# Two late reads of a channel-attention kernel, split by partitions

## The chip, the cores and the metric

One core of one Trainium2 chip runs the kernel. The metric is the device time of one execution in microseconds (us), and the median of several runs is compared.

## What is computed

x has 384 x 384 pixels of 384 channels in bf16 (113 MB). The reference takes a mean and a maximum over all pixels for each channel, sends both through the same two small layers, and scales x by the result:

```
gap = mean(x, pixels)                      # 384 values
gmp = max(x, pixels)                       # 384 values
h_a, h_m = relu(gap @ w1), relu(gmp @ w1)  # w1: 384 x 96
scale = sigmoid(h_a @ w2 + h_m @ w2)       # w2: 96 x 384
out = x * scale                            # per channel
```

No pixel can be written before every pixel was read. x does not fit into the memory beside the engines (SBUF), so there are two passes: one that reads all of x, and one that reads most of it again and writes all of it.

## The kernel before

Pixels are taken in "rows": one row is one pixel on each of 128 partitions, 768 bytes per partition. There are 1152 rows. A read of n rows brings n x 768 bytes in one piece to each partition.

*The first pass* is a list of steps written out by hand (`steps`). Lines 367 to 397 walk through it. For every read, SyncE issues the transfer (line 371); TensorE sums the rows by matmuls against ones (`sums`, line 274; for the last four reads `tail_sums`, line 290); and VectorE takes the maximum with an accumulator `acc` of eleven rows (`maximum`, line 340). VectorE takes up to six or five rows at a time, into two halves of `acc` in turn (`HALVES`), so that an instruction depends on the last but one. ScalarE and TensorE also pack some rows (lines 301 to 329); that is over by 240 us.

*The end of the first pass*, around the change: the last blocks stay in SBUF, so that the second pass need not read them again. `STAYING` gives their reads: 16 and 15 rows (stay 0), 11, 11 and 9 (stay 1), 11, 10, 8 and 5 (stay 2). Then come `LAST_HELD`: 8 rows (the late block), 2 and 6 (the kept block), 5 (the held block). After the reads up to stay 2, `turn_sums` brings the sums into place (lines 284 and 285; its copies use the room of w1 and w2, so both weights are read only afterwards, lines 399 and 400). `turn_over` transposes the late block into PSUM (line 346). Before the maximum of the six kept rows VectorE folds `acc` from eleven rows to six (`fold`); after the five held rows it folds on to one row, which TensorE transposes (line 423) and VectorE reduces (line 424). Two small products (lines 428 and 430) and a sigmoid on ScalarE (line 431) give `scale_bc`. Then SyncE also reads back eight rows (line 415) and the rows that `acc` had displaced (line 412).

*The second pass* multiplies by `scale_bc` on VectorE (line 436). ScalarE issues the stores (lines 445, 451 and 490), SyncE the reads (line 529), each into room that a store has left.

The order on each engine is the order of the program. The framework puts in the semaphore waits: a transfer signals one of eight completion semaphores (DMAHW0 to DMAHW7), taken in turn by all transfers whichever engine issues them, and waits for the one before it on the same semaphore. In the built program the five-row read of stay 2 waits for DMAHW0, the late block for DMAHW1, the kept reads for DMAHW2 and DMAHW3 and the held read for DMAHW4.

Of the kernel before, what the change touches and what calls it, by code (L numbers as in the profile page):

```python
# [39 lines left out]
FIRST_AT = (0, 104, 40, 64, 200, 176, 152)  # L40
# [12 lines left out]

FIRST_LOAD = 4
FOLD_BEFORE = 2

BETWEEN = (
    ((21, 30), (208, 48)), ((51, 21), (0, 49), (72, 21)), ((208, 51), (0, 46), (46, 34)),
# [8 lines left out]
STAYING = ((16, 15), (11, 11, 9), (11, 10, 8, 5))  # L67
# [20 lines left out]
def kernel(  # L88
# [7 lines left out]
    nc = tc.nc  # L96
    P = nc.NUM_PARTITIONS
# [9 lines left out]
    xr = x.rearrange("b h w c -> (b h w) c")  # L107
    orr = out.rearrange("b h w c -> (b h w) c")

    def rows_of(ap, block):  # L110
        first, n = block
        return ap[first * P:(first + n) * P, :].rearrange("(p n) c -> p n c", n=n)
# [7 lines left out]
    def take(n):  # L120
        nonlocal at
        at += n
        return at - n, n
# [3 lines left out]
    packed_block = take(GP * PACKED)  # L127
    late_block, kept_block, held_block = (take(sum(pieces)) for pieces in LAST_HELD)
    stay = [take(n) for _, n in SLOTS]
# [34 lines left out]
    rows = nc.alloc_sbuf_tensor_at("rows", [P, HELD_ROWS + BODY_ROWS, C], BF16, offset=RING_BYTES).ap()  # L164
# [18 lines left out]
    late = words_ps[:, 0:LATE_ROWS, :]  # L183
# [49 lines left out]
    for i in range(PACKED):  # L233
        if i in TOGETHER:
            lo = min(HOME_AT[i], D_AT[i % 2])
# [34 lines left out]
    def sums(rows, n, done, total):  # L270
        for k in range(0, n, MM_ROWS):
            g = min(MM_ROWS, n - k)
            for q in range(CQ):
                nc.tensor.matmul(  # L274
                    sum_ps[q * QP:q * QP + 1, 0:g * P],
                    lhsT=ones_bf[:, 0:1],
                    rhs=rows[:, k:k + g, q * P:(q + 1) * P],
                    start=(done + k == 0),
                    stop=(done + k + g == total),
                )  # L280

    def turn_sums():
        for r in range(MM_ROWS):
            nc.scalar.copy(out=s_sb[r % 2], in_=sum_ps[:, r * P:(r + 1) * P])  # L284
            nc.tensor.matmul(gsum_ps, lhsT=s_sb[r % 2], rhs=pick, start=(r == 0), stop=False)

    def tail_sums(rows, n, last):
        for k in range(n):
            for q in range(CQ):
                nc.tensor.matmul(  # L290
                    gsum_ps[:, q:q + 1], lhsT=rows[:, k, q * P:(q + 1) * P], rhs=ones_bf,
                    start=False, stop=(last and k == n - 1 and q == CQ - 1),
                )
# [12 lines left out]
    def test(i, what):  # L306

        if what == 2:
            test_one(high(part(i, 3), I8), 5 * i + 4)
            return  # L310
        n = G * C // 2
        a_b = homes[i][:, 0:2 * G, :].rearrange("p (r n) c -> p r (n c)", r=2).bitcast(I8)
        test_one(a_b[:, :, 2 * n * what + 1:2 * n * (what + 1):2], 5 * i + 2 * what)
        test_one(high(part(i, 2), I8)[:, n * what:n * (what + 1)], 5 * i + 2 * what + 1)

    def pack(i, half):
        n = G * C // 2
        span = slice(half * n, (half + 1) * n)
        for c in range(0, n, BANK):
            for r in range(4):  # L320
                for k, dt in enumerate((E4, E3)):
                    nc.tensor.matmul(  # L322
                        words[:, c:c + BANK], lhsT=weights[2 * r + k],
                        rhs=high(part(i, r), dt)[:, half * n + c:half * n + c + BANK],
                        start=(r == 0 and k == 0), stop=(r == 3 and k == 1),
                    )
        for r in (0, 1):
            nc.scalar.copy(out=high(part(i, r), U8)[:, span], in_=low(part(i, r + 2), U8)[:, span])  # L328
        nc.scalar.activation(  # L329
            out=part(i, 2).rearrange("p n c -> p (n c)").bitcast(U16)[:, span], in_=words,  # L330
            func=ACT.Copy, bias=32767.5,
        )

    def judge():
        nc.scalar.activation(out=test_copy, in_=tests[:, 0:NT], func=ACT.Copy, accum_out=test_sum)
        nc.scalar.copy(out=total, in_=test_sum)
        nc.tensor.matmul(bad_ps, lhsT=total, rhs=ones_bf, start=True, stop=True)

    def maximum(out_, in0, in1):
        nc.vector.tensor_tensor(out=out_, in0=in0, in1=in1, op=ALU.max)  # L340

    def turn_over(out_, rows):

        for r in range(LATE_ROWS):
            for q in range(CQ):
                nc.tensor.transpose(  # L346
                    out=out_[:, r, q * P:(q + 1) * P], in_=rows[:, r, q * P:(q + 1) * P], identity=ident_bf
                )
# [3 lines left out]
    def fold():  # L352

        n = folds[-1]
        h = n // 2
        maximum(acc[:, 0:h, :], acc[:, 0:h, :], acc[:, n - h:n, :])
        folds.append(n - h)

    done = turn = nth = 0
    for st in steps:  # L360
        if st[0] == "test":
            test(*st[1:])
        elif st[0] == "pack":
            pack(*st[1:])
        elif st[0] == "judge":
            judge()
        if st[0] != "load":
            continue
        _, block, rows, lo, hi = st
        m = hi - lo  # L370
        nc.sync.dma_start(out=rows, in_=rows_of(xr, block)[:, lo:hi, :])  # L371
        if nth < len(loads) - SUM_TAIL:
            sums(rows, m, done, TOT - tail_rows)
        else:
            tail_sums(rows, m, nth == len(loads) - 1)
        if nth == len(loads) - FOLD_BEFORE:
            fold()
        halves = HALVES if len(folds) == 1 else ((0, folds[-1]),)
        j = max(0, min(m, A - done))
        if j:  # L380
            nc.vector.tensor_copy(out=acc[:, done:done + j, :], in_=rows[:, 0:j, :])
        done += m
        if nth == len(loads) - SUM_TAIL - 1:
            turn_sums()
        while j < m:
            c, e = halves[turn % len(halves)]
            turn += 1
            e = min(e, c + m - j)
            maximum(acc[:, c:e, :], acc[:, c:e, :], rows[:, j:j + e - c, :])
            j += e - c  # L390
        if block == late_block:
            turn_over(late, rows)
        elif block == first_block:
            nc.vector.tensor_copy(out=kept_ps.bitcast(U32), in_=rows[:, 0:PSUM_ROWS, :].bitcast(U32))
            nc.vector.tensor_copy(out=kept_b.bitcast(U32), in_=rows[:, PSUM_ROWS:for_psum, :].bitcast(U32))
        nth += 1
# [23 lines left out]
    for q0, part_ps in tp_ps:  # L420
        n = part_ps.shape[1]
# [160 lines left out]
    with tc.If(bad != 0):  # L582
        for i in range(PACKED):
            for buf, lo in ((homes[i], FIRST_AT[i]), (homes_d[i], FOURTH_AT[i])):
                n = buf.shape[1]
# [33 lines left out]
```

## Time and profile before

| What | Value |
|---|---|
| median of 3 runs | 725.81 us (725.53 to 725.83) |
| the profiled execution | 725.41 us, span 723.6 us |
| first pass, up to the scale | 276.2 us |
| second pass | 447.4 us |
| VectorE busy | 564.1 us (78%) |
| ScalarE busy | 349.8 us (48%) |
| TensorE busy | 184.7 us (26%) |
| HBM read, written | 192.14 MB, 113.25 MB; 422 GB/s over the span |
| TensorE clock granted | 0.62 in the mean |

The span runs from the first to the last instruction of the profiled execution; its own time has some 1.8 us around it. A line of a timeline gives the start and the length in us, engine, line of the code, operation, output<-input, sizes and count; in brackets stands how long the engine had been idle before it and what ended that. DVE is VectorE, ACT ScalarE, PE TensorE, PEld its weight loads, SP SyncE; a q marks the engine's queue. "Landing" is the time at which a transfer's last completion event came.

### The profile page before, as it was taken

The page shows a single profiled execution, that of the slowest core. Times are in us where ns is not written, and L with a number is a line of the kernel's source. Part 1 is how long each engine was busy: PE and PEld are TensorE (multiplying, and loading weights), DVE is VectorE, ACT ScalarE, POOL GpSimd, SP SyncE. Part 2 cuts the span into 40 slices and gives each one's busy share as a digit, 9 for nine tenths or more (in the row PEclk, how much of TensorE's full clock was granted, in tenths as well). Part 3 has the DMA queues.
Part 4 walks back from the last instruction along what each step waited for, and adds up shares of the span by engine and source line. Part 5 has one row for each costly group of instructions (what it writes and reads, how often), then busy time and mean ns, then how long its engine had stood idle before and what let it go on. Part 6 is the DMA issues. An engine that isn't in the chain of part 4 may idle for free.

```text
span 723.6 us, 3882 instructions
## 1 busy us (share of the span) xinstructions
PE 184.7 (26%) x1363; PEld 74.2 (10%) x1363; DVE 564.1 (78%) x445; ACT 349.8 (48%) x251; POOL 0.7 (0%) x6
## 2 busy tenths in 40 slices
PE   5577475965867470000000000000000000001000
PEld 1222122322322140000000000000000000001000
DVE  5699899999999998797966554897888889495200
ACT  6999999997999200056230023806154442200000
POOL 0000000000000000000000000000000000000000
PEclk9888878896988555555555555555555555555555
DMA  9999999999999979999999999999999999999997
GB/s 380 434 438 435 417 442 427 429 430 432 431 426 428 426 312 356 400 433 431 433 431 431 434 428 431 434 430 435 430 429 432 437 432 430 430 433 439 442 426 339
DMA packets 20403, 305.63 MB, mean 422 GB/s; under 512 B 2624, under 2 KB 2976, under 8 KB 7200
## 3 DMA queue, kind: packets, MB, share of 16 engines
q1 hardware_dynamic: 13040, 192.14, 62.3%
q10 hardware_dynamic: 7344, 113.25, 36.6%
q8 instruction: 10, 0.16, 0.1%
q14 instruction: 9, 0.07, 0.0%
HBM read 192.14 MB, written 113.25 MB: 422 GB/s over the span
## 4 chain that ended last, share of the span: by engine, by line
DMA 63%; DVE 25%; issue 3%; PE 2%; ACT 1%; SPq 0%; DVEq 0%; ACTq 0%
DMA rows<-in_x_dram 40%; DMA out_dram<-rows 23%; DVE acc L340 16%; DVE rows L436 9%; PE words_ps L322 1%; ACT rows L328 0%; DVE acc L436 0%; SPq L371 0%; PE bank_a L274 0%; ACT rows L329 0%; ACT rows L487 0%; PE bank_a L430 0%; ACT scale_bc L431 0%; DVE small L424 0%; PE bank_a L423 0%
## 5 line engine op out<-in xcount | busy, mean ns | idle before, releaser
L436 DVE TENSOR_TENSOR rows<-rows,scale_bc 128x9216 bf16<-128x9216 bf16 (+9 forms) x56 | 230.9, 4164 | 91.2 <-DMA rows<-in_x_dram 90.0
L340 DVE TENSOR_TENSOR acc<-acc,rows 128x2304 bf16<-128x2304 bf16 (+4 forms) x227 | 245.0, 1154 | 13.9 <-DMA rows<-in_x_dram 13.6
L487 ACT COPY rows<-rows 128x1536 uint8<-128x1536 uint8 x28 | 41.3, 1476 | 204.2 <-DVE rows L436 144.8
L274 PE MATMUL bank_a<-rows,small 128*1 128x512 bf16 (+3 forms) x897 | 93.3, 466 | 80.9 <-DMA rows<-in_x_dram 76.1
L346 PE MATMUL words_ps<-ident_bf,acc 128*128 128x128 bf16 x24 | 2.7, 310 | 376.3 <-DVE acc L574 376.3
L301 ACT ACTIVATE rows<-rows 128x3072 uint8<-128x3072 int8 (+1 forms) x35 | 81.9, 2341 | 9.1 <-DMA rows<-in_x_dram 8.4
L302 ACT ACTIVATE rows<-rows 128x3072 uint8<-128x3072 uint8 (+1 forms) x35 | 82.0, 2344 | 1.1
L487 ACT COPY rows<-acc 128x1536 uint8<-128x1536 uint8 x42 | 60.5, 1473 | 18.2 <-DVE acc L473 17.7
L274 PEld LDWEIGHTS <-small 128*1 128x1 bf16 x897 | 30.6, 95 | 140.3 <-issue 118.2
L346 PEld LDWEIGHTS <-acc 128*128 128x128 bf16 x24 | 2.5, 144 | 376.7 <-DVE acc L574 376.7
L322 PE MATMUL words_ps<-rows,scale_bc 128*128 128x512 fp8e4 (+1 forms) x126 | 37.9, 414 | 9.2 <-ACT rows L329 9.2
L328 ACT COPY rows<-rows 128x1536 uint8<-128x1536 uint8 x28 | 39.7, 1468 | 0.4 <-PE words_ps L322 0.4
L322 PE MATMUL words_ps<-rows 128*128 128x512 fp8e3 (+1 forms) x126 | 35.8, 394 | 0.0
L468 DVE TENSOR_SCALAR rows<-rows 128x1536 uint16<-128x1536 uint16 x56 | 31.3, 560 | 1.9
L322 PE MATMUL words_ps<-rows,w_sb 128*128 128x512 fp8e3 x84 | 27.0, 405 | 0.0
L487 ACT COPY acc<-rows 128x1536 uint8<-128x1536 uint8 x14 | 20.5, 1466 | 0.0
L329 ACT ACTIVATE rows<-words_ps 128x1536 uint16<-128x1536 f32 x14 | 20.1, 1439 | 0.0
L322 PEld LDWEIGHTS <-scale_bc 128*128 128x128 bf16 x126 | 12.2, 103 | 30.2 <-issue 19.3
L322 PEld LDWEIGHTS <-rows 128*128 128x128 bf16 x126 | 12.9, 102 | 16.7 <-issue 3.3
L473 DVE SCALAR_TENSOR_TENSOR acc<-acc,rows 128x768 uint32<-128x768 uint32 x14 | 13.4, 959 | 0.5
L473 DVE SCALAR_TENSOR_TENSOR rows<-rows 128x768 uint32<-128x768 uint32 x14 | 13.4, 958 | 0.5
L284 ACT COPY w_sb<-bank_a 65x128 f32<-65x128 f32 x2 | 0.5, 261 | 24.5 <-PE bank_a L274 24.0
(61 smaller groups left out, 72.0 us busy)
## 6 DMA issues: line engine op xcount, KB each, us to landing
rows<-in_x_dram SPq DMA_DIRECT2D x16, 2880.0 KB, 25.4
out_dram<-rows ACTq DMA_DIRECT2D x15, 2880.0 KB, 22.8
rows<-in_x_dram SPq DMA_DIRECT2D x15, 2304.0 KB, 20.0
out_dram<-rows ACTq DMA_DIRECT2D x14, 2304.0 KB, 21.1
rows<-in_x_dram SPq DMA_DIRECT2D x4, 3072.0 KB, 31.8
out_dram<-rows ACTq DMA_DIRECT2D x2, 4608.0 KB, 46.7
rows<-in_x_dram SPq DMA_DIRECT2D x9, 768.0 KB, 16.7
rows<-in_x_dram SPq DMA_DIRECT2D x2, 3264.0 KB, 26.4
```

The costliest lines, as they stand in the source:

```text
L274: nc.tensor.matmul(sum_ps[q * QP:q * QP + 1, 0:g * P], lhsT=ones_bf[:, 0:1], rhs=rows[:, k:k + g, q * P:(q + 1) * P], start=(done + k == 0 ...
L301: nc.scalar.activation(out=out_, in_=rows, func=ACT.Square, bias=test_bias, scale=TEST_SCALE)
L302: nc.scalar.activation(out=out_, in_=out_, func=ACT.Square, bias=minus4, accum_out=tests[:, k:k + 1],)
L322: nc.tensor.matmul(words[:, c:c + BANK], lhsT=weights[2 * r + k], rhs=high(part(i, r), dt)[:, half * n + c:half * n + c + BANK], start=(r ...
L328: nc.scalar.copy(out=high(part(i, r), U8)[:, span], in_=low(part(i, r + 2), U8)[:, span])
L329: nc.scalar.activation(out=part(i, 2).rearrange("p n c -> p (n c)").bitcast(U16)[:, span], in_=words, func=ACT.Copy, bias=32767.5,)
L340: nc.vector.tensor_tensor(out=out_, in0=in0, in1=in1, op=ALU.max)
L346: nc.tensor.transpose(out=out_[:, r, q * P:(q + 1) * P], in_=rows[:, r, q * P:(q + 1) * P], identity=ident_bf)
L436: nc.vector.tensor_tensor(out=dst, in0=src, in1=scale_bc.unsqueeze(1).to_broadcast([P, n, C]), op=ALU.mult)
L468: nc.vector.tensor_scalar(out=u16(dst), in0=u16(src), scalar1=s1, scalar2=s2, op0=op0, op1=op1)
L473: nc.vector.scalar_tensor_tensor(out=u32(v), in0=u32(v), scalar=0x3F3F3F3F, in1=u32(m), op0=ALU.bitwise_xor, op1=ALU.bitwise_xor)
L487: nc.scalar.copy(out=dst, in_=src)
```

## The change

The two reads are issued in parts: the last five rows of stay 2 as 112 and four times 4 partitions, the late block's eight rows as 96, 12, 12 and 8. Every part brings the same rows to other partitions; nothing else of the first pass is written differently. (`packed` in the loop is a case that the table does not use.)

```diff
 FOLD_BEFORE = 2
+
+UNEVEN = {("stay", 2): (112, 4, 4, 4, 4), ("late", 0): (96, 12, 12, 8)}
...
+    uneven = {}
+    for (kind, i), parts in UNEVEN.items():
+        if kind == "packed":
+            uneven[packed_block, FIRST_AT[i]] = parts
+        elif kind == "stay":
+            uneven[stay[i], sum(STAYING[i][:-1])] = parts
+        else:
+            uneven[late_block, i] = parts
     done = turn = nth = 0
...
         m = hi - lo
-        nc.sync.dma_start(out=rows, in_=rows_of(xr, block)[:, lo:hi, :])
+        a = 0
+        for n in uneven.get((block, lo), (P,)):
+            nc.sync.dma_start(out=rows[a:a + n], in_=rows_of(xr, block)[a:a + n, lo:hi, :])
+            a += n
+        assert a == P
```

In the built program the nine transfers wait, in this order, for DMAHW0 (the 112), 1, 2, 3, 4 (the 4s), 5 (the 96), 6, 7 (the 12s) and 0 again (the 8); the kept and held reads that follow wait for 1, 2 and 3. TensorE's sums and transposes and VectorE's maxima of these rows wait for all parts of their read.

## The prediction

> **What bounds the kernel now.** I read the page first, then stretches around the two changed reads, then the instructions of VectorE and SyncE there one by one, and last the completion events of each transfer.
>
> The page's chain of what ended last:
>
> ```profile
> DMA 63%; DVE 25%; issue 3%; PE 2%; ACT 1%; SPq 0%; DVEq 0%; ACTq 0%
> ```
>
> Transfers lead it, but that is an average over two passes. The change sits in the last 25 us of the first pass, so that stretch decides:
>
> ```profile
> core 0: us, PE busy (x) PEld busy (x) DVE busy (x) ACT busy (x) POOL busy (x), PEclk, DMA share, GB/s
> 228.00:241.50 13.50, 6.39 (x77) 2.37 (x75) 12.69 (x12) 12.08 (x12) 0.00 (x0) 0.82 1.01 426
> 241.60:258.00 16.40, 9.33 (x67) 2.70 (x63) 16.40 (x16) 0.00 (x0) 0.00 (x0) 0.50 1.01 425
> 258.00:268.00 10.00, 7.77 (x72) 4.49 (x72) 10.00 (x11) 0.95 (x4) 0.00 (x0) 0.50 0.86 343
> ```
>
> From 241.6 us VectorE is busy without a break (16.40 of 16.40, then 10.00 of 10.00). It last waited for a read at 241.56:
>
> ```profile
> 241.56 26.48 DVE L340 TENSOR_TENSOR acc<-acc,rows 128x1920 bf16<-128x1920 bf16 x26 [0.87 <-DMA rows<-in_x_dram]
> 268.07 1.16 DVE L340 TENSOR_TENSOR acc<-acc 128x1920 bf16<-128x1920 bf16 x1
> 269.26 2.61 DVE L340 TENSOR_TENSOR acc<-acc,rows 128x2304 bf16<-128x2304 bf16 x2
> 271.90 1.54 DVE L340 TENSOR_TENSOR acc<-acc 128x1152 bf16<-128x1152 bf16 x3
> ```
>
> The line at 268.07 is the first fold (acc into acc); the two at 269.26 take the six kept rows and, from 270.71, the five held rows, the last read; 271.90 is the last three folds. Then come the scale, ready at 276.18, and the second pass. So the pass ends on a chain of VectorE work, each piece behind the one before.
>
> Are the reads late for it? In the semaphore events of the trace each read has sixteen, and the sixteenth is its landing. The reads at stake landed, and were taken by VectorE, at: five rows of stay 2: 263.42 and 264.68; late eight: 265.33 and 265.75; kept two: 265.82 and 267.49; kept six: 267.16 and 269.26; held five: 268.33 and 270.71. A waited-for landing needs about 0.09 us to become an instruction (241.47 to 241.56), so the margins are 1.2, 0.33, 1.6, 2.0 and 2.3 us. **The late block has the small one: it may land up to 265.66.**
>
> SyncE's queue (line 371 issues every read):
>
> ```profile
> 245.13 0.33 SPq L371 DMA_DIRECT2D rows<-in_x_dram  x1
> 245.55 0.38 SPq L371 DMA_DIRECT2D rows<-in_x_dram  x1
> 245.99 0.42 SPq L371 DMA_DIRECT2D rows<-in_x_dram  x1
> 248.57 0.33 SPq L371 DMA_DIRECT2D rows<-in_x_dram  x1
> 251.04 0.33 SPq L371 DMA_DIRECT2D rows<-in_x_dram  x1
> 253.54 0.33 SPq L371 DMA_DIRECT2D rows<-in_x_dram  x1
> 255.65 0.33 SPq L371 DMA_DIRECT2D rows<-in_x_dram  x1
> ...
> 266.57 1.64 SPq L400 DMA_DIRECT2D scale_bc<-in_w_dram  x1
> ```
>
> 245.99 is the five-row read, 248.57 the late block, then kept two, kept six, held five. Each of the last four starts 0.01 to 0.07 us after an earlier read landed (248.51, 251.02, 253.53, 255.58): the one eight transfers before it. The built program shows why: transfers take eight completion semaphores in turn, and one waits until the last user of its semaphore has landed. **At most eight transfers are under way.** They are issued 13 to 17 us ahead of their landing, so waits here cost nothing now.
>
> **The change part by part.**
> *Removed and added.* Two issues of 128 partitions become nine: 112+4+4+4+4 partitions of five rows, 96+12+12+8 of eight. The bytes are the same. The seven extra issues cost SyncE 0.33 to 0.42 us each, 2.3 to 2.9 us in all; SyncE waits for landings from 256 to 266 us, so this is hidden, if the new order of waits allows. VectorE gets three waiting instructions more, TensorE a few; one takes 0.02 us on VectorE's queue, which runs ahead of 1.15 us maxima: nothing.
>
> *The new order of issues.* The depth of eight is now spent on small parts. With the landings of before: 112 partitions at 245.99; the 4s at 248.57, 251.04, 253.54, 255.65; the 96 when the eleven-row read lands, 258.15, so 258.19; the 12s at 260.49 and 262.29 (landings 260.46, 262.26). The 8 waits for the 112. One partition of five rows takes an engine 149 ns (eight take 1.17 us), and every engine has seven instead of eight, so the 112 land at 263.42 - 0.15 = 263.28, and the 8 are issued at 263.31. An issue that meets an idle queue has its first packet 0.98 us later (line 415, 269.74 to 270.72); its packet takes 234 ns, and landing follows a last packet by 0.3 us (same read, 273.62 to 273.94). **The late block is complete at 263.31 + 1.0 + 0.23 + 0.3 = 264.85, earlier than before (265.33) and 0.8 us ahead of 265.66.**
>
> *What is queued behind.* Kept two, kept six and held five go out at 263.7, 264.2 and 264.6, no longer 10 us ahead. The engine that is first ended the eight-row read ahead of the change at 259.17 and has at most 3.74 us more (below), so it is empty from 262.9 on; the last one is not before 264.7. Then the thirteen rows take 13 x 0.234 = 3.04 us from about 264.8: kept two land near 265.6, kept six 267.1, held five 268.2, each within 0.3 us of before, with 1.6 us or more to spare. The weights behind them wait for TensorE (L285, 266.07) in any case. From there on the order is the same with the semaphores shifted by one, so the second pass follows the scale.
>
> *Which engines carry the parts.* No row of the trace shows it for 4, 8 or 12 partitions. The sixteen events of the late block in before run from 262.19 to 265.33, and the spread is 3.1 us in every read from 245 on: some engines are ahead, one is 1.1 us behind all others. Nearest rows: 128 and 96 partitions (weights) both left sixteen events, equal shares of 8 and 6. I take one partition to an engine. An engine with a share of everything then has 11 x 0.149 + 9 x 0.234 = 3.74 us to do after 262.26 if it is the one behind (8 each before: 3.06); one with the least has 7 x 0.149 + 6 x 0.234 = 2.45. If the slow engine has the most, the late block lands at 266.0: +0.35 us. If the least, nothing. Far end: all 48 partitions of the small parts on one engine, 1.04 + 16 x 0.149 + 1.40 + 32 x 0.234 = 12.3 us after 262.26, landing at 274.6: +8.9 us. The other end, spread as before: 0. I take 0.
>
> The Trainium skill (DMA: Bandwidth & Descriptors, on why a DMA increments its semaphore by 16) states that a transfer runs on the largest number of engines up to sixteen that divides its partitions, the lowest-numbered ones; by it the 4s share four engines, the 12s twelve, the 8 eight, and the sum stays 0 or +0.35.
>
> *Issue of odd sizes.* The only read of another size than 128 partitions at issue is w2 (96): 1.64 us against 0.33 to 0.42. Low end 0.33 each, high end 1.64 for all. If only sizes that are no power of two cost it, the second 12 end at 263.93, the 8 go at 263.98 and land at 265.52: hidden. If the 8 cost it too: 266.83, **+1.2 us**. I take the low end, nearest to the many rows.
>
> Sum: VectorE's chain 0, so 725.41 (span 723.6 and 1.8 around) + 0 = 725.41. The profiled run lies 0.40 under the median 725.81 (725.53 to 725.83); on the median the forecast is **725.8**.
>
> **The rivals.**
> *A, late block somewhat late* (slow issue, or the slow engine carries most): +0.35 to +1.2, 726.2 to 727.0. For: 1.64 us of w2, a margin of 0.33 in before. Against: 0.8 us of slack in the new order. 18%.
> *B, slower, small parts pile on few engines.* Place: the late block's tail, before VectorE's instruction at 265.75. It decides from four engines down: 11 x 0.149 + 14 x 0.234 = 4.9 us after 262.26 on the slow one, 267.2, +1.5 us; on one engine +8.9: 727.3 to 734.7. For: no row excludes it; against: equal shares in all rows seen. 16%.
> *C, slower, each added transfer pays its own latency in series:* 7 x 1.3 us (the fixed parts above) = +9 us, 735. Against: reads are issued while others move; only the 8 and what follows meet an empty queue. 3%. The Trainium skill (same page, rules for kernel authors) says many small transfers should be joined and that under 64 KB one pays mostly overhead; the 4s have 15 KB. Its price would be of this kind; here waits overlap it.
> *D, faster, the engines finish together and the pass ends earlier:* if the engine that is last has the least, 0.61 us (3.06 - 2.45) before; if all were level, at the mean of the sixteen events, 1.9 us before: 725.2 to 723.9. For: the 3.1 us spread. Against: the last rows already lie 2.3 us before VectorE takes them. 11%, of which 7% reach beyond 0.2%.
>
> **How the numbers follow.** Forecast 52%, A 18%, B 16%, C 3%, D 11%. 0.2% is 1.45 us, about what a measurement here tells from no change. Forecast, A and the small end of D (4%) are within it: 74%; B and C slower: 19%; D faster: 7%. The range holds the forecast with 0.3 us of scatter, A whole, the 0.6 us end of D and the near edge of B: 725.0 to 727.3.
>
> **What would show it.** Right: VectorE unbroken from 241.6 to 268, the last maximum near 270.7, the scale near 276.2, the 8 issued near 263.3. Wrong: a gap on VectorE before its six-row maximum at 265.75 named after a read (A, B); issues of 1 us and more at the 112, 12s and 8 (A); a last maximum before 270.5 (D); a second pass that no longer takes 447.4 us from the scale on.

## The result, and the profile after

| | before | with the change |
|---|---|---|
| median of 5 runs | 725.83 us (725.53 to 726.52) | 729.28 us (729.0 to 730.57) |
| ratio | | 1.005, 95% interval 1.0036 to 1.0065 |
| profiled execution, span | 725.41, 723.6 | 730.57, 728.6 |
| scale ready | 276.2 | 280.3 |
| second pass | 447.4 | 448.2 |

The kernel is 3.45 us slower in the median, where no change was forecast. The profiled execution is the slowest of the five; of its 5.2 us, 4.2 lie ahead of the scale. (Its second pass is 0.8 us longer than in before, 448.2 for 447.4; in the profiles of the experiments it took 447.3 to 447.9. Why is open.) This is the same view of stretches as in the prediction (the columns are length, busy time of each engine with instructions, the granted clock, the busy share of the transfer engines, and what they moved):

```profile
core 0: us, PE busy (x) PEld busy (x) DVE busy (x) ACT busy (x) POOL busy (x), PEclk, DMA share, GB/s
228.00:241.50 13.50, 6.52 (x77) 2.46 (x76) 12.69 (x12) 12.18 (x12) 0.00 (x0) 0.83 1.01 428
241.70:258.00 16.30, 9.41 (x67) 2.78 (x67) 16.26 (x16) 0.00 (x0) 0.00 (x0) 0.50 1.01 425
258.00:268.00 10.00, 4.26 (x30) 1.02 (x29) 7.12 (x8) 0.14 (x1) 0.00 (x0) 0.50 0.85 210
```

Up to 258 nothing has changed. From 258 to 268 VectorE works 7.12 us of 10 where it worked 10.00. The last two columns are the ones to read: the transfer engines are as busy as before (0.85 against 0.86), and move 210 GB/s where they moved 343. In the middle of it, the same six microseconds of before and of the changed kernel:

```profile
259.00:265.00 6.00, 3.96 (x30) 1.27 (x24) 6.00 (x7) 0.42 (x2) 0.00 (x0) 0.50 1.01 416
```

```profile
259.00:265.00 6.00, 1.96 (x15) 0.48 (x10) 4.29 (x4) 0.00 (x0) 0.00 (x0) 0.50 1.04 219
```

Busy all the time, at half the rate: **the packets themselves take longer.** The packet records say by how much. A packet of 3840 bytes (five rows to one partition) took 149 ns in before, all 256 of the five-row and held reads; in the changed kernel the median of those begun in each microsecond from 260 to 265 is 265, 269, 376, 321 and 318 ns. Packets of 6144 bytes (eight rows) went from 234 ns to 430, 424, 710, 499 and 495; these are packets of the untouched eight-row read of stay 2 and, later on, of the late block's parts.

VectorE's instructions in the changed kernel, with its idle time in brackets:

```profile
241.74 19.32 DVE L342 TENSOR_TENSOR acc<-acc,rows 128x1920 bf16<-128x1920 bf16 x18 [1.05 <-DMA rows<-in_x_dram]
261.89 2.23 DVE L342 TENSOR_TENSOR acc<-acc,rows 128x1920 bf16<-128x1920 bf16 x2 [0.83 <-DMA rows<-in_x_dram]
266.17 2.90 DVE L342 TENSOR_TENSOR acc<-acc,rows 128x1920 bf16<-128x1920 bf16 x3 [2.05 <-DMA rows<-in_x_dram]
269.55 2.29 DVE L342 TENSOR_TENSOR acc<-acc,rows 128x2304 bf16<-128x2304 bf16 x3 [0.49 <-DMA rows<-in_x_dram]
271.88 1.16 DVE L342 TENSOR_TENSOR acc<-acc 128x1920 bf16<-128x1920 bf16 x1
273.07 1.36 DVE L342 TENSOR_TENSOR acc<-acc,rows 128x2304 bf16<-128x2304 bf16 x1
274.87 1.16 DVE L342 TENSOR_TENSOR acc<-acc,rows 128x1920 bf16<-128x1920 bf16 x1 [0.44 <-ACT small L415]
```

Four new gaps, 0.83 + 2.05 + 0.49 + 0.44 = 3.81 us, and a start 0.18 us later, make up nearly all of the 4.2. The gap of 2.05 ends with a read that the change does not touch: the eight rows of stay 2, issued ahead of the 112, landed at 266.07, in before at 262.26. (The last gap is put down to ScalarE's line 415; in the built program that maximum waits for an older instruction of ScalarE, and its rows had landed at 273.20, so those 0.44 us stay unexplained.)

SyncE's issues in the changed kernel, the 96, the two 12s and the 8:

```profile
258.41 0.32 SPq L383 DMA_DIRECT2D rows<-in_x_dram  x1
261.82 0.30 SPq L383 DMA_DIRECT2D rows<-in_x_dram  x1
266.09 0.30 SPq L383 DMA_DIRECT2D rows<-in_x_dram  x1
267.08 0.27 SPq L383 DMA_DIRECT2D rows<-in_x_dram  x1
```

Each waits for the landing that the prediction named (258.35, 261.80, 266.07, and 267.07 for the 112), and none is slow to issue. The order was right; the landings were late.

### The profile page after: what moved, and what is told of

Same layout as the page of the kernel before. It is cut to its first block, busy times and chain, and to the rows that moved or that the text cites. A ratio compares the mean times of both kernels' runs of the same rounds, so it can differ in the third digit from the quotient of the medians.

```text
span 728.6 us, 3894 instructions
## 1 busy us (share of the span) xinstructions
PE 184.0 (25%) x1363; PEld 74.0 (10%) x1363; DVE 564.3 (77%) x445; ACT 349.8 (48%) x251; POOL 0.7 (0%) x6
## 4 chain that ended last, share of the span: by engine, by line
DMA 66%; DVE 17%; PE 5%; ACT 4%; issue 2%; SPq 0%; DVEq 0%; ACTq 0%
DMA rows<-in_x_dram 42%; DMA out_dram<-rows 24%; DVE acc L342 9%; DVE rows L450 8%; PE words_ps L324 3%; ACT rows L330 1%; PE bank_a L276 1%; ACT rows L303 1%; ACT rows L304 1%; ACT rows L331 1%; SPq L383 0%; PE words_ps L348 0%; DVE acc L450 0%; PE bank_b L287 0%; PE bank_b L292 0%
```

## The experiments

Three theories. **Shape:** reads on other than 128 partitions give the transfer engines shares that get in each other's way, so packets are slow, those of neighbouring reads too. **Depth:** small parts use up the eight transfers that may be under way. **Piling up:** the parts on four, eight or twelve engines load these few.

### e1_by_rows: as many transfers, cut by rows

```diff
-UNEVEN = {("stay", 2): (112, 4, 4, 4, 4), ("late", 0): (96, 12, 12, 8)}
+UNEVEN = {("stay", 2): (1, 1, 1, 1, 1), ("late", 0): (2, 2, 2, 2)}
...
-            nc.sync.dma_start(out=rows[a:a + n], in_=rows_of(xr, block)[a:a + n, lo:hi, :])
+            nc.sync.dma_start(out=rows[:, a:a + n, :], in_=rows_of(xr, block)[:, lo + a:lo + a + n, :])
```

> The same two reads in as many transfers as in the change (five and four), but cut by rows, every part on 128 partitions: five times one row, four times two rows. Shape theory (a read on other than 128 partitions gives the transfer engines shares that get in each other's way, so that packets of 768 bytes a row take about 1.8 times as long): no loss, 725.8 within 0.6 us, the scale ready at 276.2 to 276.5, packets of 36 ns per row as in whole reads, VectorE without a gap from 241.6 on. Depth theory (the small parts use up the eight transfers that may be under way, so the reads behind them start late): the loss of the change, 728.5 to 729.5, the scale near 280.

Measured: 726.26 us, 1.0004 of before (0.9995 to 1.0014). VectorE, and the six microseconds from 259:

```profile
241.57 26.49 DVE L342 TENSOR_TENSOR acc<-acc,rows 128x1920 bf16<-128x1920 bf16 x26 [1.00 <-DMA rows<-in_x_dram]
268.09 1.16 DVE L342 TENSOR_TENSOR acc<-acc 128x1920 bf16<-128x1920 bf16 x1
270.07 2.61 DVE L342 TENSOR_TENSOR acc<-acc,rows 128x2304 bf16<-128x2304 bf16 x2 [0.83 <-DMA rows<-in_x_dram]
```

```profile
259.00:265.00 6.00, 3.95 (x30) 1.22 (x24) 6.00 (x7) 0.43 (x2) 0.00 (x0) 0.50 0.82 276
```

The rate is low here as well, but read the share beside it: 0.82. The engines have nothing to do for a part of the time, and their packets are normal (36, 65 and 178 ns at the median for one, two and six rows, the same as in before). That is the depth theory's effect, and it is real: the six kept rows, issued at 263.65 and no longer at 253.54, landed at 269.98, 0.83 us too late for VectorE, and the scale was ready at 276.99. The shape theory had expected no gap and the scale by 276.5; it is right in the time and the packets, not in this. The gap is worth about a fifth of the change's 4.2 us in the profile, and is not clear of zero in the timing. Seven more transfers are not what the change costs.

### e2_stay_only and e3_late_only: one half each

```diff
-UNEVEN = {("stay", 2): (112, 4, 4, 4, 4), ("late", 0): (96, 12, 12, 8)}
+UNEVEN = {("stay", 2): (112, 4, 4, 4, 4)}      # e2
+UNEVEN = {("late", 0): (96, 12, 12, 8)}        # e3
```

> Only the five-row read is cut (112, 4, 4, 4, 4); the late block comes whole. Shape theory: packets slow down from about 259 us, when the first engines reach the 112, and the eight-row read ahead lands 2 to 4 us late, as in the change; most of the loss stays, 727.5 to 729.3. Depth theory: four extra transfers of seven, and the late block is issued near 258 us, 7 us ahead of its landing: at most half of the loss, 726 to 727.5, with packets at 234 and 149 ns.

> Only the late block is cut (96, 12, 12, 8). Shape theory: packets are normal up to about 260.5 us, slow from then on; the eight-row read and the five-row read land nearly as in before, the late block 1.5 to 3 us later than 265.3: 726.8 to 728.5. Depth theory: three extra transfers, the held read issued near 263: nothing that VectorE waits for, 725.8 within 0.6.

Measured: e2 727.24 us, 1.0023 (1.0013 to 1.0033); e3 728.12, 1.0034 (1.0025 to 1.0044). Each half loses on its own. In e2, 259 to 262 us:

```profile
256.00:259.00 3.00, 1.55 (x18) 0.49 (x13) 3.00 (x4) 0.00 (x0) 0.00 (x0) 0.50 1.01 422
259.00:262.00 3.00, 1.02 (x12) 0.26 (x9) 2.32 (x3) 0.00 (x0) 0.00 (x0) 0.50 1.07 261
```

and in e3, where the slow stretch begins a microsecond and a half later, when the first engines have done with the five rows and reach the 96 (6144-byte packets have a median of 234 ns up to 261, then 429):

```profile
259.00:262.00 3.00, 1.71 (x15) 0.42 (x10) 3.00 (x4) 0.00 (x0) 0.00 (x0) 0.50 1.06 331
262.00:265.00 3.00, 0.86 (x6) 0.22 (x6) 1.76 (x2) 0.00 (x0) 0.00 (x0) 0.50 1.01 235
```

In both, reads of 128 partitions that are under way at the same time are slow too. e2 came out a quarter of a microsecond under what the shape theory expected, e3 within it; in e3 the untouched eight-row and five-row reads landed at 264.10 and 265.95 (262.26 and 263.42 in before), which I had expected to stay, and the 96 at 268.49, 3.2 us late where 1.5 to 3 were expected. The time of e2 alone does not decide: 727.24 also lies in what the depth theory gave for it (726 to 727.5). Its packets do: 244 to 276 ns for 149, 378 to 438 ns for 234 (medians from 259 to 263 us, the five-row packets' and the eight-row packets'). The halves lose 1.6 and 2.5 us against 3.45 for the whole; the difference is within the intervals.

### e4_112_16: no part on fewer than sixteen engines

```diff
-UNEVEN = {("stay", 2): (112, 4, 4, 4, 4), ("late", 0): (96, 12, 12, 8)}
+UNEVEN = {("stay", 2): (112, 16)}
```

> The five-row read as 112 and 16 partitions; the late block whole. One extra transfer, and no part on fewer than sixteen engines. Shape theory: the slow packets are there all the same, 727 to 729. Depth theory, and the theory that the parts on four engines pile up there: no loss, 725.8 within 0.6.

Measured: 728.10 us, 1.0027 (1.0011 to 1.0042).

```profile
259.00:262.00 3.00, 1.14 (x12) 0.32 (x9) 2.44 (x3) 0.00 (x0) 0.00 (x0) 0.50 1.05 258
```

One more transfer than in before, nothing on four engines, and the same slow stretch as in e2 (258 and 261 GB/s, share 1.05 and 1.07). For the five-row read the piling up falls, and depth once more; the late block's 12s and 8 were not tried on their own. What is slow is the 112: the eight-row packets begun from 259 to 260 already have a median of 352 ns for 234, and the first engine's share of the 112, ahead of the 16, landed only at 260.62.

### e5, e6 and e7: the same, on one large read in mid-pass

The late reads are whole; the read of packed block 3, 32 rows that are read at about 100 us, is cut instead. These three ask what about a cut by partitions makes packets slow.

```diff
+UNEVEN = {("packed", 3): (64, 64)}             # e5
+UNEVEN = {("packed", 3): (32, 64, 32)}         # e6
+UNEVEN = {("packed", 3): (112, 16)}            # e7
...
-            uneven[packed_block, FIRST_AT[i]] = parts
+            uneven[packed_block, min(FIRST_AT[i], FOURTH_AT[i])] = parts
```

> The two late reads whole again; instead a read of 32 rows in the middle of the first pass (packed block 3, 24576 bytes to each partition, 912 ns a packet in before, 7.3 us in all) comes as 64 and 64 partitions. Both are powers of two, on all sixteen engines. Port theory (the 16 engines write to SBUF through 16 ports, and the partitions of one half belong to only eight of them, two engines to a port; the table is that of the Trainium skill, SBUF - State Buffer, the DMA port swizzle): half the rate, packets of about 1.8 us, the read takes some 7 us more and its landing moves by as much; 4 to 7 us of it are left at the end. Theory that only sizes that are no power of two are slow, or that the loss belongs to the end of the pass: packets of 0.91 us and 725.7.

> The same read of 32 rows as 32, 64 and 32 partitions. The 64 in the middle (32 to 95) have the same shape and the same share of four partitions an engine as in the run with two halves, but by the table of ports they reach all sixteen. Port theory: the middle part runs at 0.91 us a packet, only the outer quarters at half the rate, so about half of the loss of the two halves: landing 3.5 us late. A cause on the side of HBM, or in the shape (64 partitions, or parts as such): the same slow packets in the middle, a loss as large as with two halves or larger. No cause here: 725.7.

> The same read of 32 rows as 112 and 16 partitions: seven partitions to an engine in a row, so that engines share ports in part. Port theory: packets between 0.91 and 1.8 us, some 1.5 us in the mean as for the five rows (265 ns against 149); the read lands 3 to 5 us late. If the slow packets belong to the end of the pass: no loss, 725.7.

Measured: e5 735.34 us, 1.0131 (1.0116 to 1.0147); e6 734.72, 1.0122 (1.0107 to 1.0138); e7 734.87, 1.0124 (1.0109 to 1.0140). The read is under way between 97 and 118 us. In before:

```profile
98.00:104.00 6.00, 5.87 (x46) 2.38 (x44) 6.00 (x6) 5.97 (x5) 0.00 (x0) 1.00 1.03 442
```

In e5, the first half and the beginning of the second:

```profile
98.00:104.00 6.00, 3.98 (x21) 1.72 (x22) 4.68 (x6) 5.97 (x5) 0.00 (x0) 1.00 0.97 189
104.00:110.00 6.00, 1.89 (x27) 0.64 (x21) 6.00 (x6) 2.17 (x2) 0.00 (x0) 0.96 1.04 221
```

In e6, the first quarter, the middle part, the last quarter:

```profile
98.00:104.00 6.00, 6.00 (x47) 2.44 (x45) 6.00 (x6) 5.97 (x5) 0.00 (x0) 1.00 0.96 193
104.80:106.60 1.80, 0.00 (x0) 0.00 (x0) 1.80 (x3) 1.21 (x1) 0.00 (x0) 1.00 0.92 382
107.00:110.00 3.00, 0.00 (x0) 0.00 (x0) 2.29 (x3) 0.00 (x0) 0.00 (x0) 0.58 0.98 188
```

In e7:

```profile
98.00:104.00 6.00, 4.82 (x41) 1.89 (x38) 6.00 (x7) 5.97 (x5) 0.00 (x0) 1.00 0.99 250
104.00:110.00 6.00, 0.00 (x0) 0.00 (x0) 5.37 (x6) 2.00 (x2) 0.00 (x0) 0.83 1.16 233
```

The halves of e5 have 64 partitions, a power of two, on sixteen engines, far from the end of the pass. Still they run at 189 to 221 GB/s, with packets of 1.72 to 1.94 us (medians from 100 to 110 us) for 0.912, about twice. The middle part of e6 has the same number of partitions, the same share to an engine, and its bytes in HBM are among those of e5's two halves. Between 105 and 106 its sixteen packets have a median of 0.912 us. **Only the partitions that it writes are others, 32 to 95, and it is not slow.** So the cause of the 64s' slowness is on the side of SBUF. The Trainium skill (SBUF — State Buffer, on the DMA port swizzle) says that SBUF is reached through sixteen ports, that partitions 0 to 63 belong to eight of them, and gives some 218 GB/s for them; e5 agrees, with 189 to 221. By that table 32 to 95 reach all sixteen, and e6 agrees too. No trace here records which engine writes which partition, so that it is ports which are shared is the page's account, and not shown by these runs.

Three sizes were off. e5's read landed 11.6 us later than in before (118.09 against 106.53) where 7 were expected, since the reads ahead of and behind it are slowed with it (the one ahead landed at 103.85, before at 99.20). And e6 lost 8.9 us at the end, hardly less than e5, where half was expected: its read landed 8.2 us late (114.77). The engines are not in step, so that some are still in the outer quarters while others are in the middle, and the middle runs undisturbed for 1.8 us only. The rival had expected a loss as large as e5's, so by the time alone e6 would speak for it; the packets of the middle part speak against it. In e7 the packets took 1.1 to 1.7 us (medians from 97 to 106 us), later up to 2.9; its read landed at 115.61, 9.1 us late where 3 to 5 were expected, and the kernel lost 9.1 us. So a cut into 112 and 16 is slow in mid-pass too. But 2.9 us is over three times 0.912, and two engines that share a port would only double a packet: for 112, and for 96, sharing of ports is argued from the 64s, and how much of the slowness it makes up stays open.

### e8_four_rows_less: is VectorE the bound?

```diff
-UNEVEN = {("stay", 2): (112, 4, 4, 4, 4), ("late", 0): (96, 12, 12, 8)}
+UNEVEN = {}
...
-        a = 0
-        for n in uneven.get((block, lo), (P,)):
-            nc.sync.dma_start(out=rows[a:a + n], in_=rows_of(xr, block)[a:a + n, lo:hi, :])
-            a += n
-        assert a == P
+        short = block == stay[2] and lo == sum(STAYING[2][:2])
+        to = lo + 4 if short else hi
+        nc.sync.dma_start(out=rows[:, 0:to - lo, :], in_=rows_of(xr, block)[:, lo:to, :])
```

> All reads whole; the eight-row read of stay 2, the one ahead of the five rows, brings only its first four rows (the last four are left out: those rows keep what lay there, so the output is not the reference's). Everything behind lands 0.93 us earlier. If VectorE bounds the end of the pass: no gain, 725.7 within 0.4, the scale at 276.2. If the landing of the last reads bounds it: 0.9 us less, 724.8, the scale at 275.3.

Measured: 725.94 us, 1.0000 of before (0.9991 to 1.0009).

```profile
239.97 28.39 DVE L342 TENSOR_TENSOR acc<-acc,rows 128x1920 bf16<-128x1920 bf16 x28
268.40 1.16 DVE L342 TENSOR_TENSOR acc<-acc 128x1920 bf16<-128x1920 bf16 x1
269.59 2.61 DVE L342 TENSOR_TENSOR acc<-acc,rows 128x2304 bf16<-128x2304 bf16 x2
```

The pass runs 0.34 us late from an earlier point on (the eleven-row read landed at 258.49 for 258.15). Against that, the held read landed 0.9 us earlier than in before (267.77 - 0.34 = 267.43 for 268.33), and VectorE took it when it always did. At this place landings earlier than in before are worth nothing.

## Why the prediction was wrong, point by point

- **VectorE bounds the end of the pass, with margins of 0.33 to 2.3 us: right.** e8 shows it from one side, the gaps after the change from the other.
- **The new order of issues: right in its waits, wrong in its times.** The 8 waited for the 112 and went out 0.01 us after they landed, but at 267.08 and not at 263.31.
- **The step that failed is the duration of a packet:** "One partition of five rows takes an engine 149 ns", "its packet takes 234 ns". Both were taken from reads of 128 partitions and held for parts of 112, 96, 12 and 8. In the changed kernel packets of these sizes measured some 265 to 376 and 420 to 710 ns (medians from 260 to 265 us), those of the untouched eight-row read too. I bounded which engine gets how many packets, and what an issue costs, and never the packet, the one term that everything was multiplied with. The 112, forecast to land at 263.28, landed at 267.07; the late block, forecast to be complete at 264.85, was so at 269.38 (its 96 were last); and a read that was left alone came 3.8 us late. The trace of before has no large read of other than 128 partitions, so both ends should have been kept open. It also shows that a packet is not always 234 ns: of the read of line 415, which met idle queues, the first sixteen packets took 318 to 1118 ns. The 8, which the prediction priced with 0.23 us for the packet, landed 2.17 us after their issue and not 1.54. The Trainium skill's table of ports (SBUF — State Buffer, on the DMA port swizzle), which e5 and e6 bear out for 64 partitions, would have given a price for those, double the time, and made a rival.
- **One partition to an engine: right.** In the events of the trace each 4 has four landings, each 12 twelve and the 8 eight, besides one event half a microsecond after the issue; the 112 and the 96 have sixteen. The Trainium skill's rule for the number of engines (DMA: Bandwidth & Descriptors, on why a DMA increments its semaphore by 16), which the prediction names, agrees.
- **Issue of odd sizes: the low end was right.** 0.25 to 0.42 us for all nine parts. Rival A's price of 1.64 us does not come from the size (below).
- **Rival B, slower, had the sign but not the mechanism, and the place only in part.** That 729.28 lies in its 727.3 to 734.7 is luck. Few engines are not the trouble in the five-row read: e4, with none of those parts, loses no less than e2. VectorE's gap at B's place, before the late block's six-row maximum, is 0.49 us of the 3.81; the largest, 2.05, is ahead of it, before the untouched eight rows of stay 2. **Rival C** falls with e1: seven more transfers cost 0.6 us between the medians, not 9. **Rival D** falls with e8.
- **Kept and held reads "each within 0.3 us of before": wrong for the same reason,** and by the depth of eight besides; that part alone is e1's 0.83 us gap.

## What to carry to other kernels

A read is cheap to cut by rows and dear to cut by partitions: reads of 128 partitions kept every transfer engine at full rate here, and with parts of 112, 96 or 64 packets took mostly 1.6 to 2.5 times as long, those of the part itself and of the reads under way beside it. Which partitions a part covers counted: 64 of them, 32 to 95, were not slow. When a rate falls, read the busy share next to it: a low share with normal packets means that nothing was issued in time, a full share with a low rate means that the packets are slow. And where a change gives an operation a new shape, its duration is an unknown with two ends, not a row to copy.

## What the runs showed of the hardware beside this

- The slowdown spreads: in e4 the untouched eight-row reads on 128 partitions, the one ahead of the 112 and, by 261, the late block, had packets of 352, 388 and 465 ns (medians from 259, 260 and 261 us) for 234, from when the first engines reached the 112.
- The 1.64 us of w2's issue in before recurred in e4 (1.82 us), e5 (1.56) and e7 (1.50), and not in the others (0.43 or 0.44 in the change, e2, e3, e6 and e8, 0.77 in e1). In just those four runs a 16 KB instruction fetch began within 0.12 us of the issue (fetch and issue at 266.45 and 266.57 in before, 269.47 and 269.42 in e4, 276.41 and 276.37 in e5, 275.27 and 275.23 in e7); in the others the nearest began 0.43 us or more after it. That they belong together was not tested.
